# Attention and two expert layers on one core: two heads' scores on the two halves of the array's rows, and the last pair's transposes moved

## The chip, the cores and the metric

The kernel runs on one core of a Trainium2 chip. The metric is device time in microseconds (us), the median of several runs; lower is better. The engines in the text: PE multiplies matrices (PEld is its weight load), DVE and ACT work on vectors, POOL is the general engine, SP issues the DMA transfers.

## What is computed

An attention with a window and a few global keys feeds two expert layers, one after the other. Cut to what matters:

```python
batch, n_heads, seq, head_dim = (2, 8, 768, 64)       # n_global 8, n_local 96
scores = scale * np.matmul(q, k.transpose(0, 1, 3, 2)) + bias      # bias: slope per head times distance
scores = np.where(is_global | is_local, scores, -1000000000.0)
a = softmax(scores)                                    # (sum + 1e-09)
x = np.matmul(a, v)                                    # -> 1536 tokens x 512
h = x @ w_in;  x = np.maximum(0.01 * h, h) @ w_out     # first layer, 512 -> 2048 -> 512
h = x @ w_in2; g = P(h) / (Q(h) + 1e-06)               # second layer, P of degree 3, Q of degree 2
return g @ w_out2
```

The weights of the layers arrive as 8-byte floats and are decoded on the chip.

## The kernel before

**Precision.** A matrix product that matters is made of three matmuls: each operand is split into a high and a low part in a short float format (`qh`, `ql`, `kh`, `kl`, `xh`, `xl`, and so on), and high x high, high x low and low x high are summed in PSUM.

**Attention.** The 16 heads are handled as 8 pairs (`Pair`), two heads of 64 dimensions side by side on 128 partitions. A pair has 12 units (`Unit`): 6 blocks of 128 queries for head j = 0, then 6 for j = 1. Each block of queries sees a window of 256 key columns (128 for the first block). The score matmuls (L375 to L377) contract over 128 rows, so the q of the other head must be zero: `qz` holds for each head and each part a 128-row tile whose other 64 rows were set to zero once (`clear`). A unit then goes through `least` (DVE: bias and row minimum, from PSUM tile `sc`, two buffers), `exp` (ACT), `transposes` (PE, to `pt`), `evacuate` (ACT or DVE, to `pts`), `values` (PE, to `o`); after the last block of a head `finish` (DVE) divides and writes `xp`. The loop at L560 emits for step n the scores of unit n, the exponential of n - 1, the transposes of n - 3 and the values of n - 5. Every engine works through its own instructions in this order.

**Fillers.** After each step `fillers(n)` adds work of other pairs by tables of slots: `prep_k` and `prep_q` of the next pair (three transposes by PE, a copy by ACT, a low part by DVE or, for q, both parts by POOL), `x_out` of the pair before (its result, transposed to `xh` and `xl`), loads, and the decode of the first weights (`Decode`: two ACT steps, a sign step on DVE at L139, a shift at L148, a join on POOL at L152, then high and low part). The transposes of the fillers take a bank of the pool `hps` (two banks, tag "h").

**Expert layers.** `Layers.run` walks units u = (layer, token tile of 512, slice f of 128 hidden columns). For unit u it emits h(u), 12 matmuls at L603, then y(u - 2), 12 matmuls at L722 or L724, then the activation of u with the decode of the weights that later units need. `plan` says which pieces each unit decodes, two at a time. The decode's tile `low` takes a bank of the pool `cps` (two banks, tag "c"). The result of the last pair isn't transposed in the attention: `xp` is stored to `last_xp` in DRAM, loaded again in unit 2, and `last_x` transposes its two halves in units 4 and 6, into a bank of `cps`.

Of the kernel before, what the change touches and what calls it, by code (L numbers as in the profile page):

```python
# [25 lines left out]
def attention_moe_moe2(  # L26
# [32 lines left out]
    LOAD_Q = 8  # L59
    XOUT = (8, 11)  # L60
    BIAS = (1, 2, 4, 5, 8, 9)
    CLEAR = (2, 3, 6, 7)
# [11 lines left out]
    SIZES0 = 70  # L74
# [171 lines left out]
    def attention(wpool, w1, ffn):  # L246
        with ExitStack() as actx:
# [9 lines left out]
            def blocks(t, s):  # L257

                if s == 0:
# [4 lines left out]
            qz = [  # L264
                [
                    [bpool.tile([P, S], F32R, name=f"q{n}{j}{part}") for part in "hl"]
                    for j in range(2)
                ]
                for n in range(2)
            ]  # L270

            class Pair:
# [18 lines left out]
                def load_v(self):  # L291
                    b, h0 = self.b, 2 * self.hp
                    self.vc = apool.tile([P, 2, NB, D + 1], F32, tag="vc", name="vc")
                    self.vp = apool.tile([P, 2, NB - 1, D + 1], F32, tag="vp", name="vp")
                    for t in (self.vc, self.vp):
                        nc.gpsimd.memset(t[:, :, :, D], 1.0)
# [14 lines left out]
                def prep_k(self, s):  # L311
# [29 lines left out]
                def prep_q(self, s):  # L341
                    if s == 0:
                        self.qt = apool.tile([P, S], F32, tag="qt", name="qt", bufs=1)
                    cs = slice(s * HALF, (s + 1) * HALF)
# [15 lines left out]
            class Unit:  # L360


                def __init__(self, n):
                    self.n = n
                    self.pair = P_[n // PU]
                    self.j, self.i = divmod(n % PU, NB)
                    self.w = P if self.i == 0 else W2

                def scores(self):
                    i, w = self.i, self.w  # L370
                    c0 = 0 if i == 0 else W2 * (i - 1) + P
                    self.sc = ps.tile([P, W2], F32, tag="sc", name="sc")
                    qh, ql = (t[:, i * P : (i + 1) * P] for t in self.pair.q[self.j])
                    kh, kl = (t[:, c0 : c0 + w] for t in (self.pair.kh, self.pair.kl))
                    nc.tensor.matmul(self.sc[:, :w], qh, kh, start=True, stop=False)  # L375
                    nc.tensor.matmul(self.sc[:, :w], qh, kl, start=False, stop=False)
                    nc.tensor.matmul(self.sc[:, :w], ql, kh, start=False, stop=True)  # L377

                def least(self):
                    i, w = self.i, self.w  # L380
                    if i == 0:
                        self.pair.st[self.j] = upool.tile([P, 2, NB], F32, tag="st", name="st")
                    self.st = self.pair.st[self.j]
# [10 lines left out]
                        self.st[:, 0, i : i + 1],  # L394
                    )

                def exp(self):
                    i, w = self.i, self.w
# [5 lines left out]
                        bias=self.st[:, 0, i : i + 1],  # L404
# [19 lines left out]
                def values(self):  # L424
                    i, j, pr = self.i, self.j, self.pair
                    if i == 0:
# [38 lines left out]
            for n in range(4):  # L465
                clear(0, n // 2, n % 2)
# [579 lines left out]
```

## Time and profile before

| | us |
|---|---|
| median of 3 runs | 669.62 (669.04 to 669.88) |
| the profiled execution, whole | 670.88 |
| its span, first to last instruction | 669.1 |
| PE busy in it | 642.3 (96%) |
| DVE, ACT, POOL busy | 482.6, 447.2, 228.3 |

The span is what the trace covers; the execution's own time has 1.8 us around it. A matmul's busy time is modelled at its end, so for PE the starts of successive instructions are the better measure. Attention lies between about 8 and 126 us, the first units of the expert layers up to about 180 us, and after that both layers run to the end. The mean granted TensorE clock of the run is 0.989 of full speed.

### The profile page before, as it was taken

The numbers are of one execution on the slowest core, as the hardware profiler recorded it, in microseconds if no ns is written. First come the engines' busy times: TensorE is split into PE (matmuls) and PEld (weight loads), VectorE is DVE, ScalarE is ACT, GpSimd is POOL, SyncE is SP. The second block draws the span as 40 slices with busy tenths as digits, with TensorE's granted clock in tenths as the row PEclk, the third lists the DMA queues.
The fourth block names the chain that finished last, engine by engine and source line by source line (L and its number), as shares of the span: only waits on it lengthen the run. The fifth ranks groups of instructions, "written<-read, shape, count | busy, mean of one in ns | idle before, by whom it ended". The sixth has DMA issues, their size and how long they took to land.

```text
span 669.1 us, 9696 instructions
## 1 busy us (share of the span) xinstructions
PE 642.3 (96%) x3264; PEld 545.2 (81%) x3264; DVE 482.6 (72%) x945; ACT 447.2 (67%) x839; POOL 228.3 (34%) x226
## 2 busy tenths in 40 slices
PE   5999999967899999999999999999999999999996
PEld 4999999856788888888888888888888888788884
DVE  7788888686688565545544458898777777789784
ACT  7788888576586564545444447776677788786672
POOL 5788887143344334333000002222222222211220
PEclk9999999998899999999999999999999999999998
DMA  8467554374526676676432230000012233210001
GB/s 179 94 160 172 148 123 107 107 257 136 208 67 193 218 231 210 216 225 206 135 95 95 94 95 0 33 0 1 1 47 79 63 96 96 78 48 0 1 0 70
DMA packets 81243, 73.35 MB, mean 110 GB/s; under 512 B 51232, under 2 KB 67616, under 8 KB 81184
## 3 DMA queue, kind: packets, MB, share of 16 engines
q1 hardware_dynamic: 81184, 72.63, 36.6%
q8 instruction: 28, 0.46, 0.3%
q14 instruction: 31, 0.25, 0.1%
HBM read 60.69 MB, written 11.93 MB: 109 GB/s over the span
## 4 chain that ended last, share of the span: by engine, by line
PE 77%; DVE 7%; issue 5%; ACT 4%; POOL 4%; DMA 2%; SPq 0%; DVEq 0%; ACTq 0%; POOLq 0%
PE h L603 36%; PE y L724 19%; PE y L722 17%; POOL dec L152 1%; ACT pr L400 1%; DVE sn L386 1%; DMA w<-in_moe_w_in_dram 1%; POOL q10h L354 1%; POOL q10l L355 1%; DVE dec L148 1%; DVE kl L320 1%; PE sc L377 1%; ACT pts L417 1%; PE pt L411 1%; DVE pts L419 1%
## 5 line engine op out<-in xcount | busy, mean ns | idle before, releaser
L603 PE MATMUL h<-xh,w 128*128 128x512 f32 x768 | 255.0, 393 | 1.6 <-DVE gl L628 1.6
L603 PEld LDWEIGHTS h<-xh,w 128*128 128x128 f32 x768 | 145.7, 190 | 32.2 <-DVE gl L628 2.0
L603 PE MATMUL h<-xl,w 128*128 128x512 f32 x384 | 150.7, 393 | 0.0
L657 POOL TENSOR_TENSOR gl<-u,gh 128x512 fp32r<-128x512 f32 x44 | 57.1, 1298 | 269.0 <-PE y L724 128.0
L724 PE MATMUL y<-w,gh 128*128 128x512 f32 x384 | 126.0, 390 | 0.5 <-ACT ot L741 0.5
L722 PE MATMUL y<-gh,w 128*128 128x512 f32 x384 | 126.1, 389 | 0.0
L152 POOL TENSOR_TENSOR dec<-dec,wraw 128x512 int32<-128x512 int32 x48 | 64.0, 1343 | 100.5 <-DVE wraw L139 92.0
L724 PEld LDWEIGHTS y<-w,gh 128*128 128x128 f32 x384 | 72.1, 188 | 15.7 <-ACT ot L741 0.9
L603 PEld LDWEIGHTS h<-xl,w 128*128 128x128 f32 x384 | 72.7, 189 | 14.9
L722 PEld LDWEIGHTS y<-gh,w 128*128 128x128 f32 x384 | 72.1, 188 | 14.9
L628 DVE TENSOR_TENSOR gl<-h,gh 128x512 fp32r<-128x512 f32 x48 | 33.1, 689 | 60.0 <-ACT gh L627 60.0
L627 ACT ACTIVATE gh<-h 128x512 fp32r<-128x512 f32 x48 | 28.7, 597 | 69.8 <-PE y L722 66.4
L724 PE MATMUL y<-w,gl 128*128 128x512 f32 x192 | 75.1, 391 | 0.0
L722 PE MATMUL y<-gl,w 128*128 128x512 f32 x192 | 74.8, 389 | 0.0
L679 ACT ACTIVATE h<-h 128x512 f32<-128x512 f32 x48 | 28.6, 597 | 50.1 <-PE h L603 49.9
L623 DVE SCALAR_TENSOR_TENSOR h<-h,g 128x512 f32<-128x512 f32 x48 | 33.4, 696 | 36.6 <-ACT g L622 36.5
L400 ACT ACTIVATE pr<-sn,st 128x256 f32<-128x256 f32 (+1 forms) x96 | 47.0, 490 | 14.0 <-DVE st L386 11.4
L622 ACT ACTIVATE g<-h 128x512 f32<-128x512 f32 x48 | 28.7, 598 | 40.5 <-PE h L603 40.5
L667 DVE SCALAR_TENSOR_TENSOR w<-w,epsq,h 128x512 f32<-128x512 f32 (+1 forms) x49 | 36.3, 740 | 21.0 <-ACT h L691 20.4
L386 DVE CUSTOM_DVE_ANT_0 sn<-sc,bias 128x256 f32<-128x256 f32 (+1 forms) x96 | 37.9, 397 | 17.2 <-PE sc L377 7.6
L681 DVE SCALAR_TENSOR_TENSOR w<-h,coef,w 128x512 f32<-128x512 f32 x48 | 35.9, 749 | 18.1 <-ACT w L680 17.8
L724 PEld LDWEIGHTS y<-w,gl 128*128 128x128 f32 x192 | 36.1, 188 | 8.8 <-POOL gl L657 1.3
(143 smaller groups left out, 1231.5 us busy)
## 6 DMA issues: line engine op xcount, KB each, us to landing
wraw<-in_moe_w_in_dram SPq DMA_DIRECT2D x24, 512.0 KB, 4.5
wraw<-in_moe_w_out_dram SPq DMA_DIRECT2D x24, 512.0 KB, 4.5
scratch<-dec SPq DMA_DIRECT2D x32, 256.0 KB, 5.2
wf<-scratch SPq DMA_DIRECT2D x16, 512.0 KB, 3.4
w<-in_moe_w_in_dram SPq DMA_DIRECT2D x8, 512.0 KB, 4.2
w<-in_moe_w_out_dram SPq DMA_DIRECT2D x8, 512.0 KB, 5.0
vc<-in_v_dram SPq DMA_DIRECT2D x16, 192.0 KB, 3.3
out_dram<-ot SPq DMA_DIRECT2D x12, 256.0 KB, 2.0
```

The costliest lines, as they stand in the source:

```text
L152: nc.gpsimd.tensor_tensor(ti, ti, self.c, ALU.add)
L386: nc.vector.tensor_tensor_reduce(self.sn[:, :w], self.sc[:, :w], bias[:, 2 * self.pair.hp + self.j, b0 : b0 + w], -0.125, 3.0e38, ALU.add, ...
L400: nc.scalar.activation(self.pr[:, :w], self.sn[:, :w], AF.Exp, bias=self.st[:, 0, i : i + 1], scale=-1.0,)
L603: nc.tensor.matmul(h, wt[:, m, c * P : (c + 1) * P], xs[:, c, cs], start=c == 0 and n == 0, stop=c == NK - 1 and n == 2,)
L622: nc.scalar.activation(g, h, AF.Copy)
L623: nc.vector.scalar_tensor_tensor(h, h, 0.01, g, ALU.mult, ALU.max)
L628: nc.vector.tensor_tensor(gl, h, gh.bitcast(F32), ALU.subtract)
L657: (nc.gpsimd if on_pool else nc.vector).tensor_tensor(gl, g, gh.bitcast(F32), ALU.subtract)
L667: nc.vector.scalar_tensor_tensor(ow[:, cs], ow[:, cs], epsq, oh2[:, cs], ALU.add, ALU.mult)
L681: nc.vector.scalar_tensor_tensor(w0, h2, coef[:, 7:8], w0, ALU.mult, ALU.add)
L722: nc.tensor.matmul(ys[d], wt[:, m, ds_], gs, start=st, stop=sp)
L724: nc.tensor.matmul(ys[d], gs[:, ds_], wt[:, m, :], start=st, stop=sp)
```

## The change

Scores: `qh` and `ql` hold both heads on 128 rows, without zeros; the matmuls of head j take rows 64 j to 64 j + 63 of q and k. Units now alternate j within a block, and on even steps the loop emits the scores of two units, matmul by matmul in turn, then both `least`. Each `sc` tile is a whole bank. `st`, `o` and `finish` go by halves of three blocks and both heads. The rows of ones beside the values are set once, in two fixed pairs of tiles. `prep_k` and `prep_q` alternate, the key slots are copied in halves for every pair, the shift of the early decodes goes from DVE to POOL, and the `clear` steps are gone. The store of the last `xp` is issued by POOL, not SP. In the layers, `last_x` claims its bank at the end of units 4 and 6; the transposes and the copies are emitted in the unit after, behind its h and y; units 4 and 6 decode one piece, not two. The size checks begin at unit 68, not 70.

```diff
-    PREP0 = (("prep_k", 2, 0), ("prep_k", 4, 1), ("prep_q", 5, 0), ("prep_q", 7, 1))
-    PREP = (("prep_k", 0, 0), ("prep_k", 3, 1), ("prep_q", 5, 0), ("prep_q", 7, 1))
+    PREP0 = (("prep_k", 2, 0), ("prep_q", 4, 0), ("prep_k", 6, 1), ("prep_q", 8, 1))
+    PREP = (("prep_k", 0, 0), ("prep_q", 1, 0), ("prep_k", 4, 1), ("prep_q", 6, 1))
...
-    SIZES0 = 70
+    SIZES0 = 68
...
+                for t in v_places[n]:
+                    nc.gpsimd.memset(t[:, :, :, D], 1.0)
...
-                    for t in (self.vc, self.vp):
-                        nc.gpsimd.memset(t[:, :, :, D], 1.0)
+                    self.vc, self.vp = v_places[self.n % 2]
...
-                    if self.n == 0:
-                        self.prep_slots((0, HB) if s == 0 else (HB, NB - 1))
-                    elif s == 1:
-                        self.prep_slots((0, NB - 1))
+                    self.prep_slots((0, HB) if s == 0 else (HB, NB - 1))
...
-                    self.q = qz[self.n % 2]
-                    for j in range(2):
-                        rows = slice(j * D, (j + 1) * D)
-                        hi, lo = (t[rows, cs] for t in self.q[j])
-                        w = self.qt[rows, cs]
-                        nc.gpsimd.tensor_tensor(hi, w, zeros[rows].to_broadcast([D, HALF]), ALU.add)
-                        nc.gpsimd.tensor_tensor(lo, w, hi.bitcast(F32), ALU.subtract)
+                    hi, lo, w = self.qh[:, cs], self.ql[:, cs], self.qt[:, cs]
+                    nc.gpsimd.tensor_tensor(hi, w, zeros.to_broadcast([P, HALF]), ALU.add)
+                    nc.gpsimd.tensor_tensor(lo, w, hi.bitcast(F32), ALU.subtract)
...
-                    self.j, self.i = divmod(n % PU, NB)
+                    self.i, self.j = divmod(n % PU, 2)
+                    self.half, self.ih = divmod(self.i, HB)
...
-                    self.sc = ps.tile([P, W2], F32, tag="sc", name="sc")
-                    qh, ql = (t[:, i * P : (i + 1) * P] for t in self.pair.q[self.j])
-                    kh, kl = (t[:, c0 : c0 + w] for t in (self.pair.kh, self.pair.kl))
-                    nc.tensor.matmul(self.sc[:, :w], qh, kh, start=True, stop=False)
-                    nc.tensor.matmul(self.sc[:, :w], qh, kl, start=False, stop=False)
-                    nc.tensor.matmul(self.sc[:, :w], ql, kh, start=False, stop=True)
+                    self.sc = ps.tile([P, TT], F32, tag="sc", name="sc")
+                    rows = slice(self.j * D, (self.j + 1) * D)
+                    qh, ql = (t[rows, i * P : (i + 1) * P] for t in (self.pair.qh, self.pair.ql))
+                    kh, kl = (t[rows, c0 : c0 + w] for t in (self.pair.kh, self.pair.kl))
+                    for n, (a, b) in enumerate(((qh, kh), (qh, kl), (ql, kh))):
+                        nc.tensor.matmul(self.sc[:, :w], a, b, start=n == 0, stop=n == 2)
+                        yield
...
-                        t.shift(False)
+                        t.shift()
...
-                if unit(n):
-                    unit(n).scores()
+                if n % 2 == 0 and unit(n):
+                    for _ in zip(unit(n).scores(), unit(n + 1).scores()):
+                        pass
                     unit(n).least()
+                    unit(n + 1).least()
...
-            nc.sync.dma_start(last_xp, P_[-1].xp)
+            nc.gpsimd.dma_start(last_xp, P_[-1].xp)
...
+            def last_x(s):
+
+                steps = x_steps(cps.tile([P, TT], F32, tag="c", name="xt"), state["xp"], B - 1, NK - 1, s)
+                state["xt"] = lambda: next(steps), [lambda: next(steps), lambda: next(steps, None)]
...
-            LAST_X = (2, 4, 6)
+            LAST_X = (4, 6)
...
+                n = 1 if len(plan) in LAST_X else n
...
+                if "xt" in state:
+                    transposes, xt_tasks = state.pop("xt")
+                    transposes()
+                    tasks += xt_tasks
                 tasks += end(u - 1)
```

On PE, in the middle of a pair: before, one unit after another (`sc` scores, `pt` transposes of the probabilities, `o` values).

```order
L375 MATMUL sc<-kh,q01h 128x256 [waits DVE_49]
L376 MATMUL sc<-kl,q01h 128x256
L377 MATMUL sc<-kh,q01l 128x256
L411 MATMUL pt<-ident,pr 128x128 [waits Activation_49]
L411 MATMUL pt<-ident,pr 128x128
L432 MATMUL o<-vp,pts 128x65
L433 MATMUL o<-vc,pts 128x65
```

The same place now:

```order
L371 MATMUL sc<-kh,qh 128x256 [waits DVE_49] x2
L371 MATMUL sc<-kl,qh 128x256 x2
L371 MATMUL sc<-kh,ql 128x256 x2
L407 MATMUL pt<-ident,pr 128x128 [waits Activation_49]
L407 MATMUL pt<-ident,pr 128x128
L428 MATMUL o<-vp_131,pts 128x65
L429 MATMUL o<-vc_130,pts 128x65
```

The scores of two units stand together, their matmuls in twos (one of each head), and the transposes and values of two units follow before the next scores.

On PE, at the first transposes of the last pair's x (`xt`): before, behind h(4) and y(2) and ahead of h(5) (weights `w_2403`).

```order
L722 MATMUL y_2390<-gh,w_225 128x512
L722 MATMUL y_2390<-gl,w_225 128x512
L722 MATMUL y_2390<-gh,w_225 128x512
L196 MATMUL xt<-ident,xpb 128x128 [waits DMAHW0_49,DVE_49]
L196 MATMUL xt<-ident,xpb 128x128 x2
L603 MATMUL h<-xh,w_2403 128x512 [waits Activation_49]
L603 MATMUL h<-xl,w_2403 128x512
```

Now they stand behind h(5) and y(3) (weights `w_216`), ahead of h(6) (weights `w_2429`):

```order
L709 MATMUL y_2362<-gh,w_216 128x512
L709 MATMUL y_2362<-gl,w_216 128x512
L709 MATMUL y_2362<-gh,w_216 128x512
L196 MATMUL xt<-ident,xpb 128x128 [waits DMAHW7_49,DVE_49,PE_49]
L196 MATMUL xt<-ident,xpb 128x128 x2
L588 MATMUL h<-xh,w_2429 128x512 [waits DVE_49]
L588 MATMUL h<-xl,w_2429 128x512
```

The three transposes moved back by one h and one y. On ACT, around the copy of that transposed x: before, behind the decode of unit 4 (`dec`, `low`) and ahead of the activation of unit 5 (`g`, `gh`).

```order
L136 ACTIVATE dec<-w_2432 128x512 [waits DMAHW2_49,Activation_49]
L131 ACTIVATE low<-w_2432 128x512
L200 ACTIVATE xh<-xt 128x384 [waits PE_49]
L622 ACTIVATE g<-h 128x512 [waits PE_49,Activation_49]
L158 ACTIVATE w_2513<-dec 128x512 [waits Pool_49]
L627 ACTIVATE gh<-h 128x512 [waits DVE_49,PE_49]
```

Now:

```order
L136 ACTIVATE dec<-w_2344 128x512 [waits DMAHW0_49,Activation_49]
L131 ACTIVATE low<-w_2344 128x512
L607 ACTIVATE g<-h 128x512 [waits PE_49,Activation_49]
L200 ACTIVATE xh<-xt 128x384 [waits PE_49]
L612 ACTIVATE gh<-h 128x512 [waits DVE_49]
L158 ACTIVATE w_2483<-dec 128x512 [waits Pool_49]
```

The copy moved between the two steps of unit 5's activation, where it waits for PE's transposes.

## Rows read from the trace of the kernel before

**Rows 1.** Busy time by engine, share of the span and instructions, from the page.

```profile
PE 642.3 (96%) x3264; PEld 545.2 (81%) x3264; DVE 482.6 (72%) x945; ACT 447.2 (67%) x839; POOL 228.3 (34%) x226
```

**Rows 2.** Table of stretches: stretch, its length, each engine's busy us, clock, DMA.

```profile
7.80:25.40 17.60, 16.02 (x94) 14.77 (x94) 14.95 (x44) 12.72 (x33) 13.28 (x18) 1.00 0.84 174
66.14:79.75 13.61, 13.48 (x123) 13.27 (x122) 11.45 (x43) 11.20 (x29) 12.08 (x16) 1.00 0.63 152
...
138.00:180.00 42.00, 30.66 (x124) 24.29 (x123) 29.27 (x50) 26.70 (x49) 14.94 (x12) 0.88 0.58 200
180.00:660.00 480.00, 479.46 (x2112) 395.88 (x2111) 341.89 (x519) 312.31 (x538) 114.53 (x88) 1.00 0.29 92
```

**Rows 3.** Timeline of PE, a pair: start, duration, line, output and inputs, count.

```profile
66.14 0.30 PE L375 MATMUL sc<-kh,q00h 128*128 128x128 f32 x1
...
66.51 0.40 PE L411 MATMUL pt<-ident,pr 128*128 128x128 f32 x2
...
68.42 0.37 PE L375 MATMUL sc<-kh,q00h 128*128 128x256 f32 x1
68.62 0.28 PE L376 MATMUL sc<-kl,q00h 128*128 128x256 f32 x1
68.74 0.28 PE L377 MATMUL sc<-kh,q00l 128*128 128x256 f32 x1
68.86 0.38 PE L411 MATMUL pt<-ident,pr 128*128 128x128 f32 x2
69.08 0.33 PE L432 MATMUL o<-vp,pts 128*128 128x65 f32 x2
69.25 0.39 PE L433 MATMUL o<-vc,pts 128*128 128x65 f32 x2
...
79.75 0.31 PE L375 MATMUL sc<-kh,q10h 128*128 128x128 f32 x1
```

**Rows 4.** Timeline of PE's weight loads, one unit's scores.

```profile
68.50 0.19 PEld L376 LDWEIGHTS sc<-kl,q00h 128*128 128x128 f32 x1
68.62 0.19 PEld L377 LDWEIGHTS sc<-kh,q00l 128*128 128x128 f32 x1
```

**Rows 5.** Groups of instructions in the pair: busy us, mean ns, idle before.

```profile
L355 POOL TENSOR_TENSOR q01l<-qt,q01h 64x384 fp32r<-64x384 f32 x2 | 2.0, 1006 | 0.2
L354 POOL TENSOR_TENSOR q01h<-qt,zeros 64x384 fp32r<-64x384 f32 x2 | 1.6, 824 | 0.1
L152 POOL TENSOR_TENSOR dec<-dec,wraw 128x512 int32<-128x512 int32 x1 | 1.3, 1303 | 0.0
...
L339 POOL TENSOR_TENSOR kh<-kh,zeros 128x480 fp32r<-128x480 f32 x1 | 1.0, 985 | 0.2 <-ACT kh L318 0.2
L148 DVE TENSOR_SCALAR dec<-dec 128x512 int32<-128x512 int32 x1 | 0.9, 891 | 0.0
L339 POOL TENSOR_TENSOR kh<-kh,zeros 128x160 fp32r<-128x160 f32 x1 | 0.5, 450 | 0.0
```

**Rows 6.** Timeline of PE (idle before, releaser), and stretches at reduced clock.

```profile
140.76 0.50 PE L603 MATMUL h<-xh,w 128*128 128x512 f32 x1 [1.56 <-DVE gl L628]
153.16 0.90 PE L196 MATMUL xt<-ident,xpb 128*128 128x128 f32 x3 [6.67 <-DVE w L139]
169.07 0.53 PE L196 MATMUL xt<-ident,xpb 128*128 128x128 f32 x3 [3.11 <-DVE w L139]
153.16:156.00 2.84, 2.84 (x9) 2.36 (x10) 1.43 (x3) 0.61 (x2) 2.65 (x2) 0.50 0.28 95
169.70:173.07 3.37, 3.37 (x9) 2.60 (x8) 0.90 (x2) 0.42 (x1) 1.98 (x2) 0.50 0.37 104
```

**Rows 7.** Timeline of SP's issues and ACT's first decode after the attention.

```profile
128.74 0.34 SPq L576 DMA_DIRECT2D last_xp<-xp  x1
129.17 0.38 SPq L124 DMA_DIRECT2D wraw<-in_moe_w_out_dram  x1
133.88 0.66 ACT L136 ACTIVATE dec<-wraw 128x512 f32<-128x512 f32 x1 [2.98 <-DMA wraw<-in_moe_w_out_dram]
```

More of the change, by code (lines that the diff above doesn't have):

```diff
@@ L262, in blocks @@
                 return t[:, c0 : c0 + HB * W2].rearrange("p (i c) -> p i c", c=W2)[:, :, P:W2]
[L264 to L270, printed above, removed]
+            v_places = []
+            for n in range(2):
+                v_places.append(
+                    [bpool.tile([P, 2, c, D + 1], F32, name=f"v{w}{n}") for w, c in (("c", NB), ("p", NB - 1))]
+                )
+                for t in v_places[n]:
+                    nc.gpsimd.memset(t[:, :, :, D], 1.0)
             class Pair:
@@ L343, in prep_q @@
                         self.qt = apool.tile([P, S], F32, tag="qt", name="qt", bufs=1)
+                        self.qh, self.ql = (apool.tile([P, S], F32R, tag=n, name=n) for n in ("qh", "ql"))
                     cs = slice(s * HALF, (s + 1) * HALF)
@@ L371, in scores @@
                     c0 = 0 if i == 0 else W2 * (i - 1) + P
[L372 to L377 removed]
+                    self.sc = ps.tile([P, TT], F32, tag="sc", name="sc")
[5 more added lines that the diff above has]
+                        yield
                 def least(self):
                     i, w = self.i, self.w
[L381 to L383 removed]
+                    if self.ih == 0 and self.j == 0:
+                        self.pair.st[self.half] = upool.tile([P, 2, 2, HB], F32, tag="st", name="st")
+                    self.st = self.pair.st[self.half]
+                    self.least_at = self.st[:, 0, self.j, self.ih : self.ih + 1]
                     self.sn = upool.tile([P, W2], F32, tag="sn", name="sn")
@@ L403, in exp @@
                         AF.Exp,
-                        bias=self.st[:, 0, i : i + 1],
+                        bias=self.least_at,
                         scale=-1.0,
@@ L425, in values @@
                     i, j, pr = self.i, self.j, self.pair
-                    if i == 0:
-                        pr.o[j] = ps.tile([P, NB, D + 1], F32, tag="o", name="o")
-                    o = pr.o[j][:, i]
+                    if self.ih == 0 and j == 0:
+                        pr.o[self.half] = ps.tile([P, 2, HB, D + 1], F32, tag="o", name="o")
+                    o = pr.o[self.half][:, j, self.ih]
                     if i == 0:
@@ L435, in finish @@
                 def finish(self):
-                    j, pr, st = self.j, self.pair, self.st
-                    if j == 0:
+                    pr, st, o = self.pair, self.st, self.pair.o[self.half]
+                    if self.half == 0:
                         pr.xp = apool.tile([P, NB, P], F32, tag="xp", name="xp")
-                    nc.vector.tensor_scalar(st[:, 1], pr.o[j][:, :, D], 1e-9, None, ALU.add)
+                    nc.vector.tensor_scalar(st[:, 1], o[:, :, :, D], 1e-9, None, ALU.add)
                     nc.vector.reciprocal(st[:, 1], st[:, 1])
+                    xp = pr.xp[:, self.half * HB : (self.half + 1) * HB]
                     nc.vector.tensor_tensor(
-                        pr.xp[:, :, j * D : (j + 1) * D],
-                        pr.o[j][:, :, 0:D],
-                        st[:, 1].unsqueeze(2).to_broadcast([P, NB, D]),
+                        xp.rearrange("p i (j d) -> p j i d", j=2),
+                        o[:, :, :, 0:D],
+                        st[:, 1].unsqueeze(3).to_broadcast([P, 2, HB, D]),
                         ALU.mult,
@@ L451, in attention @@
             U = [Unit(n) for n in range(PU * len(pairs))]
-            def clear(n, j, part, on_act=True):
-                other = slice((1 - j) * D, (2 - j) * D)
-                t = qz[n][j][part][other]
-                z = zeros[other].to_broadcast([D, S])
-                if on_act:
-                    nc.scalar.activation(t, z, AF.Copy)
-                else:
-                    nc.vector.tensor_copy(t, z)
             halves = [P_[0].load(*x, HB) for x in (("qr", q), ("kr", k))]
@@ L570, in attention @@
                     unit(n - LV).values()
-                if unit(n - LV - 1) and unit(n - LV - 1).i == NB - 1:
+                if unit(n - LV - 1) and unit(n - LV - 1).ih == HB - 1 and unit(n - LV - 1).j == 1:
                     unit(n - LV - 1).finish()
@@ L862, in run @@
                     outs = []
+                    if check and u == LAST_X[0] - 2:
+                        load_last_x()
                     if check and u in LAST_X:
```

30 lines of the change are left out of this document (10 added, 20 removed).

## The prediction

> **What bounds the kernel now.** I read the busy line first [rows 1]: PE is busy 642.3 of 669.1 us, so a change pays only where it shortens PE's own work or one of PE's few gaps. Then the table by stretches [rows 2], to see where those gaps are: from 180 to 660 us PE is busy 479.46 of 480 us, a block that no edit here touches and that only shifts. In one head pair of the attention (66.14 to 79.75 us) PE is busy 13.48 of 13.61 us, while ACT has 11.20, DVE 11.45 and POOL 12.08: PE sets the pace, the others follow within 10 to 20%. In the stretch from 138 to 180 us, where the expert layers begin, PE is busy only 30.66 of 42 us at a mean granted clock of 0.88: there PE waits. So there are two places, and the change touches both.
>
> **The scores.** In the timeline of PE the starts tell the price, since the ends are modelled. A unit with 256 columns starts its three score matmuls at 68.42, 68.62 and 68.74 and the next transpose at 68.86 [rows 3]: 0.20 + 0.12 + 0.12 = 0.44 us. The 128-column unit takes 66.51 - 66.14 = 0.37. A pair has ten of the first and two of the second: 4.4 + 0.74 = 5.14 us of its 13.61. The change puts one head on array rows 0 to 63 and the other on 64 to 127, alternates their matmuls, and gives each a PSUM bank. The count of matmuls stays; what it can save is that two run at the same time. If they do fully, six matmuls take what three took: 5 x 0.44 + 0.37 = 2.57, a saving of 2.57 per pair.
>
> No row shows two matmuls side by side, nor a change between the whole array and half of its rows, so both need bounds. The weight loads: before, the loads of the score matmuls start 0.12 apart [rows 4], under a 256-column matmul each. If the two heads' loads go one after another at 0.12, a block of two units takes 6 x 0.12 + 0.08 = 0.80 instead of 0.88, and a pair saves 0.5. The quickest loads in the trace are those of the values: two loads and two matmuls between 69.08 and 69.25, so 0.085 each; six in a row take 0.51, with 0.08 of entry 0.59 a block, and the pair saves 5 x (0.88 - 0.59) + (0.74 - 0.59) = 1.6. The change of rows: at least nothing, at most the tail of a matmul that must leave the array first, 0.28 - 0.12 = 0.16 (the modelled length of L376 less its spacing), twelve times per pair: 0 to 1.9. So the saving lies between 0.5 - 1.9 = -1.4 and +2.57 per pair. I take full overlap, because the loads are hidden before too, and half of the tail, 0.08 x 12 = 0.96: 2.57 - 0.96 = 1.6, and a period of 12.0.
>
> TensorEngine Tiling in the Trainium skill ("Key Properties") says that going from one tiling to another drains the engine, which speaks against this change, since every block does it twice; it gives no figure, and no run here shows it yet. TensorE: Matmul & The Clock Gate in the Trainium skill (section "LDWEIGHTS") prices a weight load by its columns and not by its rows, columns over 1.2 GHz: by it six loads of 128 columns would be an estimated 0.64 us, with the entry 0.72 a block, and a pair would save 0.8 before the changes of rows. The trace disagrees on the size: 0.085 us for a load with its matmul.
>
> **The other engines under a period of 12.0.** DVE loses the shift of the decoded weights (L148, 0.89 us [rows 5]), which goes to POOL: 11.45 - 0.9 = 10.6. POOL's split of q goes from eight 64-row instructions to four of 128 rows with the same 384 columns; at 0.82 and 1.01 us [rows 5] that saves 2 x 1.83 = 3.7. The key slots come in halves for every pair: four more instructions, whose fixed part is 0.45 - 160 x (0.985 - 0.45)/320 = 0.18, so +0.7. The shift as a POOL multiply isn't in the trace; the join (1.30) is the nearest row, twice that the upper end. POOL: 12.08 - 3.7 + 0.7 + 1.3 = 10.4, up to 11.7. ACT keeps its 11.20, which caps any saving at 13.61 - 11.20 = 2.4. All fit under 12.0, so what moves among them costs nothing while PE is last; the ones set once (two memsets a pair), the earlier or later loads of k, q and v, and the clears gone from pair 0 are off PE's path: nothing. The first pair takes 17.60 us with PE busy 16.02 [rows 2]; its saving I put at the same 1.6, though its DVE also fills the bias tables. **Attention: 8 x 1.6 = 12.8 us**, between -11 and +19.
>
> **The start of the expert layers.** PE's three idle gaps there [rows 6]: 1.56 us before 140.76 (an h bank waits for DVE's gl), 6.67 before 153.16 and 3.11 before 169.07, both of them the transposes of the last pair's x (L196), released by DVE's sign step of the weight decode (L139). The transposes' bank rotates with the decode's "low" tiles; PE reaches the transposes right after h(u) and y(u-2), while DVE and ACT must still do the unit's activation and two decodes, which themselves start from h(u). Everything of PE stands behind. Both gaps also drop the granted clock to 0.50, the 1.2 GHz level, for 2.84 and 3.37 us of work [rows 6], of which half is lost: 1.4 + 1.7 us. Sum 1.56 + 6.67 + 3.11 + 3.1 = 14.4 us. After the change the bank is claimed at the end of unit 4 (and 6), and the transposes stand behind h(5) and y(3): 24 matmuls at 480/2112 = 0.227 us, 5.5 us of PE work, which hides the decode that they waited for. One decode less in units 4 and 6 pays for the bank. What is late next: the copy of x sits on ACT between g and gh of unit 5, so gh and gl come 12 x 0.227 = 2.7 us later; gl frees the bank of h(7), which PE reaches another 5.5 us after the transposes. That cover holds. The first gap hangs on the first decode, for which ACT waits 2.98 us on its load until 133.88; SP issued that load right behind the store of the last xp, which waited on DVE until 128.74 [rows 7]. The store moves to POOL's queue, where the next join stands behind it, and SP's loads no longer wait for xp. I count half of the 1.56. **Gain 13.5 us**, at least the part that can't come back as one unit's PE work, 13.5 - 5.5 = 8. The size checks two units earlier lie in the block where PE is full: nothing.
>
> **Sum.** 12.8 + 13.5 = 26.3. The profiled execution took 670.88 (span 669.1), 1.3 above the median of the runs, 669.62. 670.88 - 26.3 = 644.6 for it; for the median 669.62 - 26.3 = **643.3 us**.
>
> **Rivals.**
> (a) The two heads don't overlap: loads or matmuls go one after another. Per pair 0.5 less 0.96, no gain; only the 13.5 stay: **656**. For it: no row shows an overlap, and two streams share one sequence. Against it: separate banks, separate rows, and loads already hidden.
> (b) DVE sets the pace. Scores now come two units at a time into the only two banks, so PE's next scores wait until DVE has emptied both. PE's block is 12.0/6 = 2.0; where DVE has two reductions, an xl copy and a finish in a block, it needs about 0.7 + 0.55 + 0.9 = 2.2 by the spacing of such rows, and more with a decode. If 0.3 is lost in half of the blocks, the period is near 12.8: 8 x 0.8 + 13.5 = 19.9, **649.7**.
> (c) The transposes do not do what the change says: the copy of x between g and gh lets PE run into a wait one unit later, twice 2.7 us: **648.7**. Against it: the 5.5 us of cover above.
> (d) Slower: the heads don't overlap and every change of rows costs its full tail: 96 changes x 0.16 = 15.4 us more, less 13.5: **671.5**. It decides from 13.5/96 = 0.14 us a change on, with no overlap at all.
>
> **How the numbers follow.** Forecast 0.58 (its own range 638 to 648), (a) 0.14, (b) 0.16, (c) 0.08, (d) 0.04. Below 637 I leave 0.05 (changes free, ACT's cap nearly reached); above 656 half of (a) and (d), 0.11. Range 637 to 656. A measurement of this kernel can tell about 0.2% (1.3 us) from no change. Faster 0.95: all but (d), less a remainder of 0.01 for no difference; slower 0.04.
>
> **What would show it.** Right: in the timeline of a pair, score matmuls of the two heads start in twos within a few hundredths of a us, pairs come every 12 us, and no wait of xt on DVE's sign step stands between the attention and the full block; PE's clock stays at 2.4 GHz there. Score matmuls evenly 0.12 apart would show (a); PE's scores waiting for DVE's reduction (b); a PE wait on gl or on the x copy two units on (c). A first pair that stays long at the 1.2 GHz level, or ACT waiting for weight loads that now have less time to land, would make the attention term smaller.

## The result, and the profile after

The changed kernel takes 651.37 us (median of 4 runs, 650.57 to 652.42) against 669.75 us (4 runs, 669.04 to 669.98): a ratio of 0.9728, 95% interval 0.9711 to 0.9745, a gain of 18.4 us. The forecast was 643.3 with a range of 637 to 656. The time lies in the range, but the two terms of the sum missed in opposite directions: of the 12.8 us that the attention was to give only some 3 came, and the start of the expert layers gave about 16 where 13.5 had been counted.

The profiled execution took 652.42 us, its span is 650.6 us. First the busy line of the page, the row that answers to [rows 1]: PE has 7.9 us less work, and its share of the span is now 98%.

```profile
PE 634.4 (98%) x3264; PEld 529.8 (81%) x3264; DVE 474.6 (73%) x934; ACT 440.8 (68%) x833; POOL 211.0 (32%) x220
```

The table of stretches of the changed kernel (stretch, its length, each engine's busy time, granted clock, DMA share, GB/s) answers to [rows 2]: one pair of the attention and the start of the expert layers.

```profile
64.62:78.07 13.45, 13.05 (x122) 11.66 (x121) 10.64 (x42) 11.18 (x29) 9.74 (x15) 1.00 0.69 163
118.00:180.00 62.00, 62.00 (x288) 51.58 (x288) 50.42 (x88) 47.68 (x85) 26.00 (x21) 1.00 0.52 179
```

The second half is as the prediction drew it: between 118 and 180 us PE has no gap, and the clock is 1.00, the 2.4 GHz level, where before 11 us were idle. The first row is not. A pair takes 13.45 us, not 12.0; before it took 13.61. PE is still the engine that is last (13.05 of 13.45 us), with DVE at 10.64, ACT at 11.18 and POOL at 9.74 behind it.

The waits of PE over the whole span (who waits, for whom: us in total, times, longest) show the same. No wait of the expert layers is left; two are new, in the second and the fourth row (`st` stands for DVE's reduction of the scores), while a wait of 0.7 us for POOL's low part of q is gone.

```profile
PE h L306 <- DMA qr<-in_q_dram: 5.5, 1, 5.5
PE h L306 <- DVE xl L202: 2.2, 5, 0.6
PE sc L371 <- DVE kl L318: 1.3, 1, 1.3
PE sc L371 <- DVE st L382: 0.8, 2, 0.7
```

The timeline of PE over one block of two units (start, duration, line, output and inputs, count) answers to [rows 3]:

```profile
59.78 0.39 PE L429 MATMUL o<-vc,pts 128*128 128x65 f32 x2
60.10 0.39 PE L371 MATMUL sc<-kh,qh 64*128 64x256 f32 x2
60.32 0.28 PE L371 MATMUL sc<-kl,qh 64*128 64x256 f32 x2
60.44 0.28 PE L371 MATMUL sc<-kh,ql 64*128 64x256 f32 x2
60.65 0.44 PE L407 MATMUL pt<-ident,pr 128*128 128x128 f32 x2
60.92 0.33 PE L428 MATMUL o<-vp,pts 128*128 128x65 f32 x2
61.09 0.39 PE L429 MATMUL o<-vc,pts 128*128 128x65 f32 x2
61.32 0.50 PE L196 MATMUL h<-ident,xp 128*128 128x128 f32 x3
61.65 0.38 PE L407 MATMUL pt<-ident,pr 128*128 128x128 f32 x2
61.87 0.33 PE L428 MATMUL o<-vp,pts 128*128 128x65 f32 x2
```

The two heads do run at the same time. Each "x2" row is one matmul of each head, 3 to 4 ns apart. Six score matmuls take 60.10 to 60.65 = 0.55 us; two units took 2 x 0.44 = 0.88 before [rows 3]. But what stands around them became dearer. From the values to the first score there are 60.10 - 59.78 = 0.32 us (0.19 before: 69.25 [rows 3] to 69.44). From the last score to the transpose there are 0.21 (0.12 before), inside the 0.55. The first transposes behind the scores take 60.92 - 60.65 = 0.27 (0.22 before, and 61.65 to 61.87 here where no score stands ahead). The next score rows of the kernel before, the last two with a gap between them:

```profile
69.44 0.37 PE L375 MATMUL sc<-kh,q00h 128*128 128x256 f32 x1
69.65 0.28 PE L376 MATMUL sc<-kl,q00h 128*128 128x256 f32 x1
70.06 0.39 PE L377 MATMUL sc<-kh,q00l 128*128 128x256 f32 x1
```

To sum this up, give each row of PE's timeline the time to the next row's start, over one pair. (What it costs to enter the scores then lies in the row ahead of them.)

| us in a pair | before, 66.14 to 79.75 | after, 64.62 to 78.07 | difference |
|---|---|---|---|
| scores | 5.55 | 3.25 | -2.30 |
| values | 4.12 | 5.32 | +1.20 |
| transposes of the probabilities | 2.42 | 2.74 | +0.32 |
| transposes of k, q and x (in threes) | 1.52 | 2.14 | +0.62 |
| sum | 13.61 | 13.45 | -0.16 |

The gain in the scores is nearly all taken back by their neighbours. The pieces:

- **Overlap.** The scores save 2.30, and 2.30 + 6 x 0.09 = 2.84 without the dearer exit; 0.29 of it is a gap that one score of the old pair had (70.06 - 69.65 = 0.41 from one start to the next where 0.12 is usual). That leaves 2.55: the 2.57 of the prediction.
- **Changes of rows.** Entry from the values 5 x (0.308 - 0.195) = 0.57, entry from the transposes once 0.47 - 0.25 = 0.22, exit 6 x 0.09 = 0.54, first transposes behind the scores 6 x 0.05 = 0.30. Sum 1.63 for twelve changes, 0.136 each. The prediction took 0.08.
- **New neighbours.** The transposes of k, q and x used to stand right ahead of scores; five of the six now stand ahead of the probabilities' transposes, and from their start to the next row's there are 0.33 instead of 0.25: 5 x 0.08 = 0.40. (0.33 for three is the rate of the probabilities' transposes, 0.22 for two; it is the 0.25 ahead of whole-row scores that stands out.)
- **A new wait.** One row of the pair is `67.28 … L306 … h<-ident,qr`, shown with the sixth experiment below: 0.79 us from the row ahead of it instead of 0.22, 0.57 lost.

2.57 + 0.29 - 1.63 - 0.40 - 0.57 = 0.26, where 0.16 is measured; 0.1 stays unassigned.

**The start of the expert layers.** The first h matmul stood at 120.30 us and stands at 117.99; from there to the end of the span it is 669.1 - 120.30 = 548.8 before and 650.6 - 117.99 = 532.6 after. So 16.2 us were won behind the attention and 2.3 in it. The idle time before PE's rows [rows 6] accounts for 1.56 + 6.67 + 3.11 = 11.3. The rest shows in the groups of instructions (busy us, mean ns | idle before, releaser), of before in this fence:

```profile
L603 PE MATMUL h<-xh,w 128*128 128x512 f32 x768 | 255.0, 393 | 1.6 <-DVE gl L628 1.6
L603 PE MATMUL h<-xl,w 128*128 128x512 f32 x384 | 150.7, 393 | 0.0
L724 PE MATMUL y<-w,gh 128*128 128x512 f32 x384 | 126.0, 390 | 0.5 <-ACT ot L741 0.5
L196 PE MATMUL xt<-ident,xpb 128*128 128x128 f32 x6 | 1.4, 361 | 9.8 <-DVE w L139 9.8
```

and of the changed kernel in this one:

```profile
L588 PE MATMUL h<-xh,w 128*128 128x512 f32 x768 | 252.7, 390 | 0.0
L588 PE MATMUL h<-xl,w 128*128 128x512 f32 x384 | 149.4, 389 | 0.0
L711 PE MATMUL y<-w,gh 128*128 128x512 f32 x384 | 125.5, 389 | 0.0
L196 PE MATMUL xt<-ident,xpb 128*128 128x128 f32 x6 | 1.0, 272 | 0.0
```

The same matmuls are 2.3 + 1.3 + 0.5 + 0.4 = 4.5 us shorter. About 3.1 of it is the work at the 1.2 GHz level, half of 2.84 + 3.37 us [rows 6]: the h matmuls start 0.43 us apart there and 0.23 apart now. The rest is not taken apart here; rows right behind a gap are slower too (0.34 instead of 0.23 from the one at 140.76 to the next). A wait of 0.5 near the end is gone as well: 11.3 + 4.5 + 0.5 = 16.3, against 16.2 measured.

### The profile page after: what moved, and what is told of

Same layout as the page of the kernel before. It is cut to its first block, busy times and chain, and to the rows that moved or that the text cites. A ratio compares the mean times of both kernels' runs of the same rounds, so it can differ in the third digit from the quotient of the medians.

```text
span 650.6 us, 9650 instructions
## 1 busy us (share of the span) xinstructions
PE 634.4 (98%) x3264; PEld 529.8 (81%) x3264; DVE 474.6 (73%) x934; ACT 440.8 (68%) x833; POOL 211.0 (32%) x220
## 4 chain that ended last, share of the span: by engine, by line
PE 93%; DVE 4%; issue 1%; DMA 1%; ACT 0%; SPq 0%; DVEq 0%
PE h L588 40%; PE y L711 20%; PE y L709 20%; PE sc L371 4%; PE pt L407 3%; PE o L429 2%; PE o L428 2%; PE h L306 2%; DVE sn L382 1%; DVE xl L202 1%; DMA ints<-in_n_global_dram 1%; PE h L196 0%; DVE w L161 0%; PE o L426 0%; DVE xp L438 0%
## 5 line engine op out<-in xcount | busy, mean ns | idle before, releaser
L588 PEld LDWEIGHTS h<-xh,w 128*128 128x128 f32 x768 | 144.2, 188 | 29.7
L711 PEld LDWEIGHTS y<-w,gh 128*128 128x128 f32 x384 | 72.1, 188 | 14.8
L588 PEld LDWEIGHTS h<-xl,w 128*128 128x128 f32 x384 | 72.1, 188 | 14.8
L652 DVE SCALAR_TENSOR_TENSOR w<-w,epsq,h 128x512 f32<-128x512 f32 (+1 forms) x49 | 36.2, 740 | 20.9 <-ACT h L676 20.3
L382 DVE CUSTOM_DVE_ANT_0 sn<-sc,bias 128x256 f32<-128x256 f32 (+1 forms) x96 | 34.8, 399 | 18.1 <-PE sc L371 9.2
```

The source lines that it names most:

```text
L382: nc.vector.tensor_tensor_reduce(self.sn[:, :w], self.sc[:, :w], bias[:, 2 * self.pair.hp + self.j, b0 : b0 + w], -0.125, 3.0e38, ALU.add, ...
L588: nc.tensor.matmul(h, wt[:, m, c * P : (c + 1) * P], xs[:, c, cs], start=c == 0 and n == 0, stop=c == NK - 1 and n == 2,)
L652: nc.vector.scalar_tensor_tensor(ow[:, cs], ow[:, cs], epsq, oh2[:, cs], ALU.add, ALU.mult)
L711: nc.tensor.matmul(ys[d], gs[:, ds_], wt[:, m, :], start=st, stop=sp)
```

## The experiments

Each kernel ran beside the kernel before on the same chip; the ratios are to that. Medians of the kernel before in these runs: 670.24 (experiments 1, 3, 4 and 6), 670.09 (2), 670.13 (5, 7, 8 and 9), 669.61 (10), 670.31 (11).

**1 and 2. Each half of the change alone.** In the first, the attention is that of the kernel before, and only the last pair's transposes get their bank a unit ahead:

```diff
-            LAST_X = (2, 4, 6)
+            LAST_X = (4, 6)
...
+                n = 1 if len(plan) in LAST_X else n
...
+                if "xt" in state:
+                    transposes, xt_tasks = state.pop("xt")
+                    transposes()
+                    tasks += xt_tasks
```

> The kernel before with the changed transposes of the last pair alone (bank claimed a unit ahead, emitted behind the next h and y, one decode in units 4 and 6); the store of the last xp stays on SP and the attention is untouched. Theory A (the whole gain of the change is here): the gaps of 6.67 and 3.11 us and 3.1 us at the lower clock go, the gap of 1.56 stays, since SP's loads still stand behind the store: 669.7 - 13 = 656.7 us, or 655 if that gap goes too. Theory B (attention and transposes share the gain of 18.3 about equally): 660 us or more.

656.89 us (4 runs, 655.38 to 658.97), ratio 0.9815 (0.9784 to 0.9845): 13.4 us, nearly three quarters of the gain. Its PE waits behind 100 us:

```profile
PE h L603 <- DVE gl L628: 0.9, 1, 0.9
PE y L726 <- ACT ot L743: 0.5, 1, 0.5
...
```

The two waits for the sign step are gone, that on gl is not. The other half alone, attention as changed and the last pair's transposes as before (the first diff turned round, on the changed kernel, with the store on SP's queue):

> Edit: the other half of the change alone: attention as changed (both heads' scores on 64 rows, the ones set once, k and q by turns), but the last pair's transposes, their place and the store on SP's queue as before. Theory A (the attention saves only 2.3 us to the first matmul of the expert layers, and the start of those layers saves about 16): 666 to 669 us, and the three gaps before the transposes and the first units' h are there again, 10 us or more in all. Theory B (the two halves lean on each other, and the attention alone is worth 5 us or more): 665 us or less.

665.96 us (6 runs, 665.66 to 666.68), ratio 0.9942 (0.993 to 0.9954): 4.1 us, at the edge between the two theories, nearer to A. Its PE waits, first and fifth row:

```profile
PE xt L196 <- DVE w L139: 9.8, 2, 6.6
...
PE h L588 <- DVE gl L613: 1.1, 1, 1.1
```

The gaps are back, as A has it. 13.4 + 4.1 = 17.5 of the 18.4: the halves nearly add up (the store on POOL's queue is in neither). Of the 4.1 some 0.9 lie behind the first h matmul, from which the end of the span is 664.0 - 116.09 = 547.9 us away here and 548.8 before; the attention is worth about 3, not 12.8. The traces bound it: the first h matmul starts at 120.30 and 119.12 with the old attention (before, experiment 1), and at 117.99, 117.45, 116.09 and 116.03 with the new one (after, experiments 9, 2 and 5), 2.8 us between the means.

What scatters is the first pair, whose length is 16.8, 15.8, 14.9 and 14.8 us in these four, under the same attention. The same two score rows show why, in the changed kernel (first fence) and in this experiment (second):

```profile
17.05 0.41 PE L371 MATMUL sc<-kl,qh 64*128 64x256 f32 x2
17.27 0.41 PE L371 MATMUL sc<-kh,ql 64*128 64x256 f32 x2
```

```profile
16.68 0.28 PE L371 MATMUL sc<-kl,qh 64*128 64x256 f32 x2
16.80 0.28 PE L371 MATMUL sc<-kh,ql 64*128 64x256 f32 x2
```

At the start of each of these traces PE's rows lie nearly twice as far apart (0.22 us here instead of 0.12), although the granted clock of 12 to 20 us reads 1.00 in both traces. They close up near 20.3 us in the changed kernel and near 18.4, 16.2 and 15.5 in experiments 9, 2 and 5, in the order of the lengths above. What sets that moment is not shown. The seven pairs behind the first are free of it: from the second pair's first score to the first h matmul there are 95.24 and 95.40 us with the old attention, and 93.37, 93.79, 93.41 and 93.42 with the new one, about 1.8 us less.

**3. What a change of rows costs.** The scores on all 128 rows, in the changed order; nothing else moves:

```diff
-                    rows = slice(self.j * D, (self.j + 1) * D)
+                    rows = slice(0, P)
```

> The changed kernel with score matmuls over all 128 rows, same order, same count, same banks. It sums both heads' products, so its scores are not the reference's; only the time is read. No overlap, and no change of tiling. Theory A (the heads overlap fully, but going to half rows and back costs PE about 0.27 us per block of two units): a block's scores go from 0.55 to 0.80 us, but the 0.12 on entry and the 0.13 behind go away, net +0.09 x 48 blocks = +4: 655.5 us. Theory B (the changes of rows are nearly free, and DVE and ACT set the pace of the pair): PE has slack to lose, 651 to 653 us. Theory C (changes free and PE still last): +0.36 x 48 = 17: 668 us.

655.24 us (4 runs, 655.17 to 655.92), ratio 0.9783 (0.9758 to 0.9808), as theory A gave. PE's timeline of one block:

```profile
63.17 0.39 PE L429 MATMUL o<-vc,pts 128*128 128x65 f32 x2
63.36 0.49 PE L371 MATMUL sc<-kh,qh 128*128 128x256 f32 x2
63.69 0.40 PE L371 MATMUL sc<-kl,qh 128*128 128x256 f32 x2
63.92 0.40 PE L371 MATMUL sc<-kh,ql 128*128 128x256 f32 x2
64.16 0.38 PE L407 MATMUL pt<-ident,pr 128*128 128x128 f32 x2
64.38 0.33 PE L428 MATMUL o<-vp,pts 128*128 128x65 f32 x2
```

With whole rows the entry is 63.36 - 63.17 = 0.19, the transposes behind take 0.22, and the last matmul of a block is as long as the others. All three extras are gone, and with them the overlap: six matmuls take 0.80 us. From the values' last row to the row behind the first transposes it is 64.38 - 63.17 = 1.21 here and 60.92 - 59.78 = 1.14 in the changed kernel: half rows save 0.07 a block, since 0.25 of overlap is paid for with 0.18 at the edges.

**4. Taking the overlap away by order.** Three matmuls of one head, then three of the other:

```diff
-                    for _ in zip(unit(n).scores(), unit(n + 1).scores()):
-                        pass
+                    for g in (unit(n).scores(), unit(n + 1).scores()):
+                        list(g)
```

> The changed kernel, half rows as in it, but the three matmuls of one head first and then the three of the other, so that they cannot run beside each other except at the border; the changes of tiling stay. Theory A: a block's scores go from 0.55 to about 0.55 + 2 x 0.12 or 3 x 0.12 (two or three of the six no longer hidden), so +0.24 to +0.36 x 48 = +12 to +17: 663 to 668 us. Theory B (DVE and ACT set the pace): 651 to 656 us. If the two heads had not overlapped in the first place: 651 us.

652.23 us (4 runs, 650.56 to 653.06), ratio 0.9732 (0.9703 to 0.9762): no change, so the expectation failed. The timeline says why:

```profile
61.07 0.39 PE L371 MATMUL sc<-kh,qh 64*128 64x256 f32 x2
61.29 0.29 PE L371 MATMUL sc<-kl,qh 64*128 64x256 f32 x2
...
```

The rows are still in twos: the fourth matmul of the program starts 10 ns behind the first and ahead of the second, where the second of the changed kernel starts 3 to 4 ns behind its first. So each half of the array got its own next matmul, whichever order the program had within a block. The experiment therefore did not take the overlap away, and it says nothing about its worth; the alternating order of the change is not what brings it.

**5. The place of the store.** The last xp is stored from SP's queue, as before the change:

```diff
-            nc.gpsimd.dma_start(last_xp, P_[-1].xp)
+            nc.sync.dma_start(last_xp, P_[-1].xp)
```

> The changed kernel with the store of the last xp issued by SP again, so the first weight loads of the layers stand behind it. Theory A (what the store's new queue gives is the one gap of about 1 us before the third h): 652.4 us, with a PE wait on DVE's gl there. Theory B (the loads' earlier start carries more, because the decode runs late for several units): 654 us or more. If it gives nothing: 651.4.

652.12 us (5 runs, 651.91 to 652.75), ratio 0.973 (0.9716 to 0.9743). PE's timeline has the wait on gl again:

```profile
135.89 0.50 PE L588 MATMUL h<-xh,w 128*128 128x512 f32 x1 [0.99 <-DVE gl L613]
```

So the store is what had held up the load of `wraw` and through it this h. The load that stood right behind the store was issued at 129.17, 8.9 us behind the first h matmul [rows 7]; in this experiment it is issued at 124.90, again 8.9 behind (116.03), and ACT waits 2.43 us for it. In the changed kernel it goes out 3.2 us ahead of the first h matmul, and ACT does not wait:

```profile
114.77 0.46 SPq L124 DMA_DIRECT2D wraw<-in_moe_w_out_dram  x1
```

The wait of about 1 us is what theory A gave; in the median the store's place is worth under 1 us, within the uncertainty.

**6. Half as many changes of rows.** Four units' scores at a time, each head's two blocks in the halves of its bank:

```diff
-                    self.sc = ps.tile([P, TT], F32, tag="sc", name="sc")
+                    if i % 2 == 0:
+                        self.pair.sc[self.j] = ps.tile([P, 2, W2], F32, tag="sc", name="sc")
+                    self.sc = self.pair.sc[self.j][:, i % 2]
...
-                if n % 2 == 0 and unit(n):
+                if n % 4 == 0 and unit(n):
+                    for m in (n, n + 2):
+                        for _ in zip(unit(m).scores(), unit(m + 1).scores()):
```

> The changed kernel with the scores of four units at a time (two blocks of both heads, each head's two blocks in the two halves of its bank), so 3 instead of 6 changes to half rows per pair; six buffers for sn. Theory A: 24 blocks fewer pay the 0.27 us: -6.4, 645 us, if the four reductions in a row on DVE don't hold up its copies. Theory B: no gain, 651 us or more, since DVE now reduces four units in a row before it copies anything.

647.34 us (4 runs, 647.01 to 647.74), ratio 0.9662 (0.9638 to 0.9687). The same kernel ran once more (this run was meant to hold experiment 11's second edit too, and does not): 647.88 us (5 runs, 647.71 to 648.91). The direction is A's, the size is not reached. The stretch of one pair:

```profile
60.50:73.80 13.30, 12.25 (x123) 11.31 (x122) 10.85 (x42) 11.09 (x30) 9.47 (x15) 1.00 0.71 160
```

PE's work in a pair fell by 0.80, 13.05 to 12.25; six changes fewer at 0.136 are 0.82. But the period only fell by 0.15, because the new wait grew. Here it stands in the changed kernel's timeline (first fence) and in that of four units at a time (second):

```profile
67.28 0.55 PE L306 MATMUL h<-ident,qr 128*128 128x128 f32 x3 [0.40 <-DVE xl L202]
```

```profile
64.15 0.55 PE L306 MATMUL h<-ident,qr 128*128 128x128 f32 x3 [0.98 <-DVE xl L202]
```

**7. The new wait.** The two h banks go round between the transposes of k, q and x. The change put q's first transposes into slot 1 of a pair; their bank is that of the last x_out piece, started in slot 10 of the pair before, and DVE's xl (0.55 us) is queued there behind a decode. Move that piece one slot ahead:

```diff
-    XOUT = (8, 10)
+    XOUT = (8, 9)
```

> The changed kernel with the second half of the transposed result one slot earlier (slot 9 instead of 10), so that its low part is done before the next pair's first slots. Theory A (PE still sets the pace, and each pair loses 0.4 us where the next q's transposes wait for that low part to leave their bank): -0.4 x 7 = -2.8: 648.6 us, and the wait of PE on DVE's xl gone. Theory B (DVE and ACT set the pace of a pair): the wait moves elsewhere, 651.4.

648.4 us (5 runs, 647.92 to 650.59), ratio 0.9677 (0.9658 to 0.9695), as A gave. The stretch of one pair, and all waits of PE:

```profile
62.35:75.18 12.83, 12.83 (x121) 11.48 (x120) 10.54 (x43) 11.04 (x30) 9.74 (x15) 1.00 0.73 168
```

```profile
PE h L306 <- DMA qr<-in_q_dram: 5.4, 1, 5.4
PE sc L371 <- DVE kl L318: 1.3, 1, 1.3
PE sc L371 <- DVE st L382: 0.7, 1, 0.7
```

The wait is gone, the period is 12.83, and PE is busy in all of it.

**8. Both, with the pieces too early.** Four units at a time, and the x_out pieces in slots 7 and 9:

```diff
-    XOUT = (8, 10)
+    XOUT = (7, 9)
```

> Scores of four units at a time, and the transposed result in slots 7 and 9. With four units at a time PE works 12.25 us of a pair's 13.30 and waits 1.0 for the bank that DVE's xl holds. Theory A: that wait goes, -1.0 x 7 = -7 from 647.3: 640 us. Theory B (ACT, with 11.05 busy, or DVE's four reductions in a row come next): the period stays above 12.8, 644 us or more.

649.53 us (5 runs, 648.97 to 651.34), ratio 0.9699 (0.9683 to 0.9715): a miss by 9 us of theory A, and in B's range. The wait has only moved, to ACT's copy of q, which still holds the bank one slot behind q's transposes in slot 6:

```profile
71.43 0.55 PE L196 MATMUL h<-ident,xp 128*128 128x128 f32 x3 [1.36 <-ACT qt L343]
```

**9 and 10. Two edits of the change that should cost or bring nothing.** Units 4 and 6, where the transposes take their bank, with two decodes each again:

```diff
-                n = 1 if len(plan) in LAST_X else n
```

> The changed kernel with two decoded pieces in units 4 and 6 again; the transposes stay behind the next h and y. Theory A (their place in PE's order is what removed the waits, since 5.5 us of matmuls now cover the decode): no change, 651.4 us. Theory B (the bank has to be paid for with a decode): PE waits again for DVE's sign step, some of the 6.7 and 3.1 us return, 654 to 660 us.

651.04 us (5 runs, 650.67 to 651.98), ratio 0.971 (0.9697 to 0.9723): the transposes still do not wait, so it was their place in PE's order that took the gaps away and not the decode left out. And the shift of the decoded weights on DVE:

```diff
-                        t.shift()
+                        t.shift(False)
```

> Edit: the shift of the decoded weights goes back from POOL to DVE everywhere; all else as changed. Theory A (PE is last in the attention by 13.05 of 13.45 us a pair, DVE has 10.6 of it): 0.9 us more on DVE in a pair stays off PE's path except through the copy of x_out's low part, which DVE makes and q's transposes wait for; 651.4 to 653 us. Theory B (the move of the shift was part of the gain, since DVE sets when the score banks come free): 654 us or more.

651.27 us (5 runs, 650.68 to 651.69), ratio 0.9725 (0.9711 to 0.9739): nothing, as an edit is worth that moves 0.9 us between two engines that are not last.

**11. Both, in the right place.** Four units at a time, with the pieces in slots 8 and 9 (the two diffs of experiments 6 and 7 together):

> Edit: the scores of four units at a time (half of the changes of rows) and, in the same kernel, the second x_out piece of the previous pair in slot 9 instead of 10. Theory A (a change of rows costs about 0.26 us a block, and the wait of q's transposes on the low part of x_out is one of place): PE's work in a pair is 12.2 to 12.4 us as with four units, the wait on xl of 1.0 us a pair is gone, periods come near 12.3 to 12.6, and the time is 640 to 643 us. Theory B (below a period of 12.8 another engine sets the pace and a wait turns up elsewhere, as on ACT's copy of q with the pieces in 7 and 9): the period stays at 12.8 or above and the time is 645 to 650 us.

643.21 us (5 runs, 642.98 to 645.02), ratio 0.9602 (0.9587 to 0.9617), just above what A gave, and better than both kernels. The stretch of a pair, and all of PE's waits:

```profile
59.27:71.71 12.44, 12.23 (x121) 11.34 (x120) 11.10 (x42) 11.09 (x30) 9.52 (x15) 1.00 0.75 175
```

```profile
PE h L306 <- DMA qr<-in_q_dram: 5.4, 1, 5.4
PE sc L373 <- DVE kl L318: 1.3, 1, 1.3
PE h L306 <- DVE kl L318: 0.3, 1, 0.3
```

The period is 12.44 and the first h matmul starts at 108.32 us: 12 us ahead of the kernel before, about what the prediction had expected of the attention. Of these, 3.1 lie in the first pair; the seven pairs behind it take 86.4 us instead of 95.2, a saving of 8.9 where 7 x 1.6 = 11.2 had been counted. Most of the overlap was there to be had; it needed half as many changes of rows and a free bank. Counted as in the table above, the pair has scores 2.86, values 4.92, transposes of the probabilities 2.64 and those of k, q and x 2.02 us. That the first pair is shorter too (14.1 us against 16.8 in the profile of the changed kernel) is at least in part the scatter named under experiment 2: its rows close up near 15 us.

## Why the prediction was right and where it was wrong

The time fell into the range, the sign was right, and the forecast itself was 8.1 us too fast. By its own steps:

- **What bounds the kernel.** Right. PE is last in the pair before and after, and the gaps at the start of the expert layers were real time: removing them alone gave 13.4 us.
- **The heads overlap.** Right. Rows in twos, 2.55 us of saving per pair against 2.57. Rival (a) falls.
- **The change of rows: the step that failed.** The prediction bounded it by 0 to 0.16 us and took the half, 0.08; it is 0.136, so twelve of them cost 1.63 a pair where 0.96 stood, 5.4 us over eight pairs. The bound was good, the middle of it was not: 0.136 is most of the tail it came from (a matmul's modelled length of 0.28 less its spacing of 0.12). That the cost hangs on the changes is shown from both sides: without them it vanishes (experiment 3), and six fewer take 0.80 off a pair (experiment 6). TensorEngine Tiling (Array Packing) in the Trainium skill ("Key Properties") says that a change of tiling mode drains the engine; the runs agree that a change costs time, and put a size to it.
- **What stands next to what.** Missing from the sum. The change also puts the transposes of k, q and x ahead of other transposes; 0.40 a pair, 3.2 us over eight. The prediction priced a block of scores by its own rows and let its neighbours keep their old spacing.
- **Banks that are shared with moved work.** Missing too. "The earlier or later loads of k, q and v … nothing" held for the loads, but q's transposes moved to slot 1 and met the x_out piece that holds their bank: 0.57 us in four pairs and 0.78 in a fifth, 3.1 in all, of which the table of waits shows 2.2 as idle time. Experiment 7 shows it by its removal: 3.0 us.
- **Sum of the attention.** 12.8 less 5.4, 3.2 and 3.1 is 1.1, and the 0.29 a pair of a gap in the old pair brings it to 3.4; measured 2.3 in the profiled execution, 2.8 between the means of six traces. Without the first pair the same terms give 11.2 - 4.7 - 2.8 - 3.1 + 2.0 = 2.6, against 1.9 in the profiled execution; most of the difference is one block at 87.21 us, which takes 0.6 us more than its like because PE waits there for a bank of scores.
- **The first pair.** "A first pair that stays long" was among the signs of a smaller attention term, and it showed: 16.8 us in the profiled execution, up to 2.0 more than in other runs of the same attention. The prediction tied it to the 1.2 GHz level; PE's rows do lie nearly twice as far apart there, but the granted clock reads 1.00.
- **Slips in its sums.** Loads one after another would have saved 5 x 0.08 - 0.06 = 0.34 a pair, not 0.5; rival (a) calls 0.5 less 0.96 no gain, which is a loss of 0.46 a pair; and 14.4 less half of 1.56 is 13.6, not 13.5. None of them decided anything.
- **Rival (b), DVE as the pace.** Falls. PE waits 0.8 us in all for a bank of scores, and at a period of 12.44 (experiment 11) DVE has 11.10 and the table of waits has none for a bank of scores. That its time, 649.7, lies nearer to the measured one than the forecast does is chance: the pairs were long by PE's own rows and by a bank of transposes.
- **Rival (c), a wait two units on.** Falls. No row of PE between 118 and 180 us waits, and the cover of 5.5 us held.
- **Rival (d), slower.** Its price per change was nearly met (0.136 where it began to decide at 0.14), but it also needed that the heads do not overlap, and they do.
- **The start of the expert layers.** Mechanism right, size short by 2.7. The work at the 1.2 GHz level is the 3.1 that were counted. The first gap went whole (1.56, half had been counted), a wait of 0.5 near the end went too, and the rest, about 1.4, lies in matmul time outside that level, which the sum did not have. That the store's move takes the first gap away is shown by experiment 5. The wait near the end stands in the two traces whose size checks begin at unit 70 (before, experiment 1) and in none of those with 68, so the size checks, put at nothing, may be what removed it; that was not tried alone.
- **What moved among the other engines.** Nothing, as costed: the shift on DVE or POOL (experiment 10), one decode or two (experiment 9). The shift as a POOL multiply took 1.04 us, below its bounds of 1.3 to 2.6.

What stays open: why three transposes take 0.33 us ahead of other transposes and 0.25 ahead of whole-row scores, and what sets the moment at which PE's rows close up in the first pair.

## What to carry to other kernels

When a step is made quicker by another mode of the matrix engine, price the edges before the step: count how often the mode changes, put the whole tail of a matmul at each change until a row says less, and ask first how many steps can stand between two changes. Price the neighbours of every moved row by rows in which they stand side by side, and for each transposition or copy moved to another slot ask which work last held the buffer that it will get. An idle gap in front of a full block is the safer gain: it came back whole, and with it what the lower clock behind it had cost.

## What the runs showed of the hardware

- A change between 128 and 64 rows costs on the way in 0.11 us (0.31 against 0.20 from the values, on average over a pair) and on the way out 0.09 at the last matmul and 0.05 at the first one behind. With whole rows in the same order (experiment 3) all three vanish.
- Matmuls on the upper and the lower 64 rows start within 3 to 10 ns of each other, whichever order the program gives them within a block (experiment 4). TensorEngine Tiling (Array Packing) in the Trainium skill ("Key Properties") says that tiles operate independently; the trace agrees, and shows that this reaches over two instructions of the other tile that stand ahead in the program.
- The weight loads of six score matmuls lie in 0.55 us with the matmuls, because they go in twos as well: they start at 60.10, 60.21 and 60.32, one of each head. The prediction's estimate of 0.72 for such a block, from TensorE: Matmul & The Clock Gate in the Trainium skill ("LDWEIGHTS"), put the six one after another; the trace does not bear that out.
